# Retention with adapters: batches on opposite partition halves, and 64x64 causal score tiles

## The chip, the cores and the metric

The kernel runs on one core of one Trainium2 chip. The metric is the device time of one execution in microseconds. Three runs of the kernel before gave 205.89, 206.98 and 207.31 us; the median is 206.98 us.

## What is computed

For 8 batches, 8 heads, 576 tokens and a head size of 64, the first part is retention: `scores = (q kᵀ) / 8`, every score multiplied by `gamma_h ** (i - j)` where token j is not after token i and by zero elsewhere, and the result multiplied by v. `gamma_h = 1 - 2 ** (-5 - h)`. The 8 heads of a token side by side form a row x of 512.

The second part is a mixture of adapters on the 4608 rows x: `logits = x @ w_gate` (8 experts), the two largest logits are turned into two weights by a softmax over the two, and the output is `x + sum over the two experts of weight * (x @ A[e]) @ B[e]`, where A[e] is 512 x 16 and B[e] is 16 x 512. All inputs and the output are float32.

## The kernel before, in words

Retention is computed in chunks of 128 tokens, four full ones and a last one of 64. Because the decay factorises, `gamma ** (i - j)` is split: q carries `gamma ** i` (times the scale 1/8), v carries `gamma ** -j`, and what earlier chunks contribute is a 64 x 64 state P per batch and head, multiplied by `gamma ** 128` from chunk to chunk.

The work is cut into *units*: one chunk of one pair of batches. A *quad* is one chunk of four batches, so two units, and is what is loaded at a time: chunk 0 of batches 0 to 3, chunk 0 of batches 4 to 7, chunk 1 of batches 0 to 3, and so on. There are 16 full units and 4 half ones (the chunk of 64). In a full unit the 128 tokens lie on the 128 partitions, and the two batches lie beside each other in the free dimension.

For each unit the stages, with their lines, are:

- T (`stage_T`, L204): 16 transposes of q (L229) and 16 of k (L229), each of 64 tokens by two heads, into PSUM tiles `pt_q` and `pt_k`. VectorE moves q out and multiplies it by `aqp`, the decay and the scale (L241); ScalarE copies k out (L250).
- S (`stage_S`, L264): 16 score matmuls of kT (64 x 128) with qT (64 x 128) into four tiles `ps_s` (L291), and four VectorE products with the triangular mask `tri` into `rt` (L302). The whole 128 x 128 square of a chunk is computed, and its upper triangle is multiplied by zero.
- O (`stage_O`, L323): from the second chunk on, 16 matmuls of the state P with qT, into `px` (L359); and 16 matmuls of k with v over 128 tokens into `pu` (L373). VectorE adds the old state (L387) and GpSimd multiplies by `gamma ** 128` (L388).
- R (`stage_R`, L395): 16 matmuls of v with rt on top of `px` (L408), copied out by ScalarE as xT (L417). xT is the transposed row x.
- Z (`stage_Z`, L440): 8 matmuls of xT with A and w_gate side by side (L447) into `pz`, then the router on VectorE and ScalarE (L460 to L479), which ends with `zc`.
- B, X, Y (L501, L487, L523), for the unit before: 16 transposes of xT back into `po` (L512), two of zc into `pzt` (L493) with a ScalarE copy (L498), four matmuls with B on top of `po` (L533), four ScalarE copies to `osb` (L543) and the stores (L548).

GpSimd multiplies v by its decay in place (`scale_v`, L197). A half unit has two batches on opposite partition halves, 64 tokens each, and does the same stages in smaller shapes (L341, L426, L437).

A float32 matmul appears in the trace as two instructions, a transpose as one. A tile form such as 64*128 is the number of rows and columns of the TensorE array that an instruction uses; instructions on different parts of the array can overlap.

The order of the work is written out in the loop at the end of the kernel (L561 to L576):

```python
        if t % 2 == 0:
            issue(t // 2 + 2)
        stage_S(t)
        if t + 1 < NU:
            scale_v(t + 1)
        stage_O(t)
        stage_R(t)
        if t + 1 < NU:
            stage_T(t + 1)
        if t > 0:
            stage_B(t - 1)
            stage_X(t - 1)
        stage_Z(t)
```

A scheduler of the language puts each engine's instructions into their order, mostly the written one, and inserts the waits. All PSUM tiles come from one pool `pp` of eight banks. All loads of q, k and v and all stores are issued from SyncE's queue (SP), in one order: the loads of a quad are issued two quads ahead (`issue`, L158), into one of three sets of buffers. A full quad is three DMAs of 1 MB (L127); the first quad is loaded in two halves of 512 KB per tensor, with the constants and the adapters' weights (L101, L105) between them; the last chunk's DMAs write 64 partitions each (L148).

Of the kernel before, what the change touches and what calls it, by code (L numbers as in the profile page):

```python
# [18 lines left out]
def kernel(  # L19
# [17 lines left out]
    NP = B // 2  # L37
    NFULL = S // 128
    LH = S - 128 * NFULL
    QUAD = 4  # L40
    NQ = B // QUAD

    scale = 1.0 / float(np.sqrt(Dh))
    gam = 1.0 - 2.0 ** (-5.0 - np.arange(H, dtype=np.float64))
    jj = np.arange(128, dtype=np.float64)

    ident32_np = np.eye(128, dtype=np.float32)
    tri_np = (jj[None, :] >= jj[:, None]).astype(np.float32)
    j64 = np.arange(128) % 64
    i64 = np.arange(64)  # L50
    trih_np = (i64[None, :] >= j64[:, None]).astype(np.float32)
    aqp_np = np.zeros((128, HP, 128), dtype=np.float32)
    g128_np = np.zeros((128, HP), dtype=np.float32)
    for hp in range(HP):
        for ho in range(2):
            g = gam[2 * hp + ho]
            aqp_np[64 * ho : 64 * ho + 64, hp, :] = scale * g ** jj[None, :]
            g128_np[64 * ho : 64 * ho + 64, hp] = g**128.0
    gv_np = np.stack([gam[h] ** (-jj) for h in range(H)], axis=1).astype(np.float32)
    gvh_np = np.stack([gam[h] ** (-j64.astype(np.float64)) for h in range(H)], axis=1).astype(  # L60
        np.float32
    )
    i64_np = np.concatenate([np.eye(64), np.eye(64)], axis=0).astype(np.float32)
    first_np = i64_np
    rest_np = np.concatenate(
        [ident32_np, tri_np, trih_np, gv_np, gvh_np, g128_np], axis=1
    ).astype(np.float32)
    NPK = rest_np.shape[1]
    dr_first = nc.inline_tensor(first_np, "c_first")
    dr_rest = nc.inline_tensor(rest_np, "c_rest")  # L70
    dr_aqp = nc.inline_tensor(aqp_np, "c_aqp")
# [5 lines left out]
    pp = ctx.enter_context(tc.tile_pool(name="pp", bufs=8, space=bass.MemoryType.PSUM))  # L77

    id64 = cpool.tile([128, 64], FP32, tag="id64", name="id64")
# [5 lines left out]
    aqp = cpool.tile([128, HP, 128], FP32, tag="aqp", name="aqp")  # L85
    ident32 = pack[:, 0:128]
    tri = pack[:, 128:256]
    trih = pack[:, 256:320]
    gv = pack[:, 320 : 320 + H]
    gvh = pack[:, 320 + H : 320 + 2 * H]  # L90
    g128 = pack[:, 320 + 2 * H : 320 + 2 * H + HP]

    AW = []
    for par in range(2):
        AW.append(cpool.tile([128, HP, ER + E], FP32, tag=f"AW{par}", name=f"AW{par}"))
    Bcat = cpool.tile([128, Dm], FP16, tag="Bcat", name="Bcat")
    ident16 = cpool.tile([128, 128], FP16, tag="ident16", name="ident16")

# [12 lines left out]

    nat = {}

    def issue_full(c, qd, split):
        tiles = []
        for src, tag in ((q, "q32"), (k, "k32"), (v, "v32")):
            tiles.append((src, iop.tile([128, QUAD * H, Dh], FP32, tag=tag, name=tag)))
        parts = ((0, 2), (2, 4)) if split else ((0, 4),)
        for lo, hi in parts:
            for src, tl in tiles:  # L120
                if split and lo == 0 and src is k:
                    nc.sync.dma_start(out=aqp, in_=dr_aqp.ap())
                if split and lo == 0 and src is v:
                    nc.sync.dma_start(out=pack, in_=dr_rest.ap())
                if split and lo == 2 and src is q:
                    load_moe()
                nc.sync.dma_start(  # L127
                    out=tl[:, lo * H : hi * H, :],
                    in_=src[
                        QUAD * qd + lo : QUAD * qd + hi, :, 128 * c : 128 * c + 128, :  # L130
                    ].rearrange("b h j d -> j (b h) d"),
                )
        for half in range(2):
            nat[(c, 2 * qd + half)] = [
                tl[:, half * 2 * H : half * 2 * H + 2 * H, :] for _, tl in tiles
            ]

    def issue_half(qd):

        s0 = 128 * NFULL  # L140
        tiles = []
        for src, tag in ((q, "q32"), (k, "k32"), (v, "v32")):
            tiles.append((src, iop.tile([128, QUAD * H, Dh], FP32, tag=tag, name=tag)))
        for slot in range(2):
            for src, tl in tiles:
                for par in range(2):
                    b = QUAD * qd + 2 * slot + par
                    nc.sync.dma_start(  # L148
                        out=tl[64 * par : 64 * par + LH, slot * H : slot * H + H, :],
                        in_=src[b, :, s0 : s0 + LH, :].rearrange("h j d -> j h d"),  # L150
                    )
            nat[(NFULL, 2 * qd + slot)] = [
                tl[:, slot * H : slot * H + H, :] for _, tl in tiles
            ]

    quads = [(c, qd) for c in range(NFULL + 1) for qd in range(NQ)]

    def issue(n):  # L158
        if n < len(quads):
            c, qd = quads[n]  # L160
            if c < NFULL:
                issue_full(c, qd, n == 0)
            else:
                issue_half(qd)
# [155 lines left out]
    def col(full, b, ho):  # L320
        return (ho ^ b) if full else ho
# [289 lines left out]
```

## Time and profile before

| what | value |
|---|---|
| median of three runs | 206.98 us |
| the profiled execution's own time | 207.16 us |
| its span, first to last instruction | 205.1 us |
| TensorE matmul busy | 183.8 us (90%), 3564 instructions |
| TensorE weight loads | 166.2 us, 3564 instructions |
| VectorE busy | 108.7 us (53%) |
| ScalarE busy | 76.6 us (37%) |
| GpSimd busy | 59.6 us (29%) |
| DMA, q1 (loads and stores) | 38.50 MB, 68.0% of 16 engines' span |

The profile is of one execution. PE is TensorE's matmuls, PEld its weight loads, DVE VectorE, ACT ScalarE, POOL GpSimd, SP SyncE. The rows of digits cut the span into 40 slices; a digit is a busy share in tenths, and PEclk is the TensorE clock that was granted. In the chain that ended last, a line gives the start, the length, the engine, the tile written and the source line with the number of instructions; the chain goes from each piece of work to what released it. In the timeline an x32 stands for 32 instructions merged into one line, and the length goes to the modelled end of the last one. In the table of stretches, each line has the stretch, its length, the busy time of PE, PEld, DVE, ACT and POOL with their instruction counts, the granted clock, the DMA share and GB/s.

### The profile page before, as it was taken

The page shows a single profiled execution, that of the slowest core. Times are in us where ns is not written, and L with a number is a line of the kernel's source. Part 1 is how long each engine was busy: PE and PEld are TensorE (multiplying, and loading weights), DVE is VectorE, ACT ScalarE, POOL GpSimd, SP SyncE. Part 2 cuts the span into 40 slices and gives each one's busy share as a digit, 9 for nine tenths or more (in the row PEclk, how much of TensorE's full clock was granted, in tenths as well). Part 3 has the DMA queues.
Part 4 walks back from the last instruction along what each step waited for, and adds up shares of the span by engine and source line. Part 5 has one row for each costly group of instructions (what it writes and reads, how often), then busy time and mean ns, then how long its engine had stood idle before and what let it go on. Part 6 is the DMA issues. An engine that isn't in the chain of part 4 may idle for free.

```text
span 205.1 us, 8039 instructions
## 1 busy us (share of the span) xinstructions
PE 183.8 (90%) x3564; PEld 166.2 (81%) x3564; DVE 108.7 (53%) x286; ACT 76.6 (37%) x206; POOL 59.6 (29%) x60
## 2 busy tenths in 40 slices
PE   0476989799999999999999999999999999999950
PEld 0376969598999999999999999999999899888830
DVE  0226364937374746465656565656565655456630
ACT  2022324153525262625252525253434344454430
POOL 1144323521818202727202720643222402000000
PEclk9999999999999999999999999999999999999997
DMA  5989999799998988991799969756545311222222
GB/s 114 277 109 246 249 243 280 194 290 290 253 319 245 261 249 274 284 297 36 220 286 254 266 215 293 213 145 179 150 118 158 96 51 60 101 79 76 58 47 61
DMA packets 57442, 39.14 MB, mean 191 GB/s; under 512 B 30912, under 2 KB 52672, under 8 KB 57408
## 3 DMA queue, kind: packets, MB, share of 16 engines
q1 hardware_dynamic: 57264, 38.50, 68.0%
q8 instruction: 28, 0.46, 0.9%
q0 software_dynamic: 144, 0.13, 0.4%
q14 instruction: 6, 0.05, 0.1%
HBM read 29.32 MB, written 9.44 MB: 189 GB/s over the span
## 4 chain that ended last, share of the span: by engine, by line
PE 72%; SPq 9%; DVE 7%; DMA 5%; ACT 3%; issue 1%; ACTq 0%
PE pz L447 16%; PE px L408 12%; PE ps_s L291 12%; PE pu L373 6%; PE px L359 6%; PE pt_q L229 5%; DMA k<-in_k_dram 5%; PE po L512 4%; SPq L127 4%; PE pt_k L229 4%; PE po L533 3%; DVE rt L302 2%; PE px L426 2%; ACT osb L543 2%; SPq L101 2%; PE pzt L493 2%
## 5 line engine op out<-in xcount | busy, mean ns | idle before, releaser
L197 POOL TENSOR_TENSOR v<-v,pack 128x512 f32<-128x512 f32 x36 | 36.6, 1042 | 28.0 <-DMA v<-in_v_dram 28.0
L417 ACT COPY xT<-px 128x512 f32<-128x512 f32 x32 | 18.7, 585 | 66.0 <-PE px L408 66.0
L388 POOL TENSOR_TENSOR P<-pn,gdec 128x512 f32<-128x512 f32 x16 | 20.3, 1271 | 75.3 <-DVE pn L387 58.9
L302 DVE TENSOR_TENSOR rt<-ps_s,pack 128x512 f32<-128x512 f32 x64 | 39.7, 682 | 4.2 <-PE ps_s L291 4.2
L291 PE MATMUL ps_s<-qT,kT 64*128 64x128 f32 (+1 forms) x640 | 37.4, 275 | 1.2 <-ACT kT L250 1.2
L447 PE MATMUL pz<-AW,xT 128*128 128x136 f32 x288 | 37.8, 283 | 0.4 <-ACT zT L498 0.4
L291 PEld LDWEIGHTS ps_s<-qT,kT 64*128 64x128 f32 (+1 forms) x640 | 33.7, 184 | 5.3 <-DVE lg L460 3.4
L241 DVE TENSOR_TENSOR qT<-pt_q,aqp 128x512 f32<-128x512 f32 x32 | 20.6, 686 | 31.1 <-PE pt_q L229 31.1
L408 PE MATMUL px<-rt,v 128*64 128x128 f32 x512 | 34.1, 275 | 1.8 <-DVE rt L302 1.7
L447 PEld LDWEIGHTS pz<-AW,xT 128*128 128x128 f32 x288 | 34.7, 190 | 0.6 <-ACT zT L498 0.5
L543 ACT COPY osb<-po 128x256 f32<-128x256 f32 x72 | 23.1, 375 | 25.8 <-PE po L533 25.8
L408 PEld LDWEIGHTS px<-rt,v 128*64 128x64 f32 x512 | 29.0, 137 | 3.8 <-DVE rt L302 2.5
L250 ACT COPY kT<-pt_k 128x512 f32<-128x512 f32 x32 | 17.2, 589 | 19.2 <-PE pt_k L229 19.2
L460 DVE COPY lg<-pz 128x16 f32<-128x16 f32 (+1 forms) x20 | 3.5, 173 | 35.0 <-PE pz L447 35.0
L229 PE MATMUL pt_q<-id,q 64*128 64x64 f32 x288 | 13.6, 234 | 6.7 <-DMA q<-in_q_dram 6.7
L373 PE MATMUL pu<-v,k 128*64 128x64 f32 x512 | 18.9, 225 | 0.0
L373 PEld LDWEIGHTS pu<-v,k 128*64 128x64 f32 x512 | 16.5, 137 | 2.7 <-issue 2.1
L229 PEld LDWEIGHTS pt_q<-id,q 64*128 64x128 f32 x288 | 10.8, 142 | 9.6 <-issue 9.4
L229 PE MATMUL pt_k<-id,k 64*128 64x64 f32 x288 | 12.8, 228 | 3.4 <-DMA k<-in_k_dram 3.4
L473 DVE SCALAR_TENSOR_TENSOR cm<-lg,m,sg 128x8 f32<-128x8 f32 x36 | 9.9, 294 | 8.8 <-ACT sg L468 8.8
L229 PEld LDWEIGHTS pt_k<-id,k 64*128 64x128 f32 x288 | 10.9, 143 | 3.8 <-issue 1.7
L359 PE MATMUL px<-qT,P 64*64 64x128 f32 x384 | 13.2, 275 | 0.0
(34 smaller groups left out, 139.9 us busy)
## 6 DMA issues: line engine op xcount, KB each, us to landing
out_dram<-osb SPq DMA_DIRECT2D x32, 256.0 KB, 3.2
q<-in_q_dram SPq DMA_DIRECT2D x2, 512.0 KB, 5.0
k<-in_k_dram SPq DMA_DIRECT2D x2, 512.0 KB, 6.0
v<-in_v_dram SPq DMA_DIRECT2D x2, 512.0 KB, 5.4
q<-in_q_dram SPq DMA_DIRECT2D x8, 128.0 KB, 3.4
k<-in_k_dram SPq DMA_DIRECT2D x8, 128.0 KB, 3.3
v<-in_v_dram SPq DMA_DIRECT2D x8, 128.0 KB, 4.1
out_dram<-osb SPq DMA_DIRECT2D x8, 128.0 KB, 2.4
```

Source lines behind the costliest of these rows:

```text
L197: nc.gpsimd.tensor_tensor(out=v32[:, b * H : b * H + H, :], in0=v32[:, b * H : b * H + H, :], in1=g.unsqueeze(2).broadcast_to((128, H, Dh) ...
L229: nc.tensor.matmul(ps[r][:, hp, b, :] if full else ps[r][:, hp, :], lhsT=src[sl, b * H + 2 * hp : b * H + 2 * hp + 2, :], rhs=id64[sl, :], ...
L241: nc.vector.tensor_tensor(out=o, in0=ps[r], in1=aqp[:, :, 64 * r : 64 * r + 64] .unsqueeze(2) .broadcast_to((128, HP, 2, 64)), op=ALU.mult,)
L291: nc.tensor.matmul(o, lhsT=kT[sl, hp, b, :], rhs=qT[sl, hp, b, :], start=(a == 0 and (b == 0 or not full)), stop=True, skip_group_check=True,)
L302: nc.vector.tensor_tensor(out=r.rearrange("p a b i -> p (a b) i"), in0=ps[ho].rearrange("p a b i -> p (a b) i"), in1=tri.unsqueeze(1).broa ...
L359: nc.tensor.matmul(px[b][64 * cc : 64 * cc + 64, hp, :], lhsT=P[bp][64 * ho : 64 * ho + 64, hp, b, :], rhs=qT[64 * ho : 64 * ho + 64, hp, ...
L373: nc.tensor.matmul(pu[64 * ho : 64 * ho + 64, hp, b, :], lhsT=s["k"][:, b * H + h, :], rhs=s["v"][:, b * H + h, :], start=(hp == 0 and b = ...
L388: nc.gpsimd.tensor_tensor(out=pf, in0=pn, in1=gdec.rearrange("p a b d -> p (a b d)"), op=ALU.mult,)
L408: nc.tensor.matmul(px[b][64 * cc : 64 * cc + 64, hp, :], lhsT=s["v"][:, b * H + h, :], rhs=rt[h][:, b, :], start=(c == 0 and hp == 0), sto ...
L417: nc.scalar.copy(out=xt, in_=px[b])
L447: nc.tensor.matmul(pz[:, b, :], lhsT=xts[b][:, dt, :], rhs=AW[b][:, dt, :], start=(dt == 0), stop=(dt == HP - 1), skip_group_check=True,)
L543: nc.scalar.copy(out=osb[:, b, :, cc ^ b, :], in_=po[cc][:, b])
```

## The change

The kernel is rewritten around another layout. The two batches of a full unit now lie on opposite partition halves: batch b has partitions 64b to 64b+63. A chunk of 128 tokens is two parts e = 0, 1 (early and late 64 tokens), each in a tile of its own. A unit is still two batches of one chunk (of the four batches of a quad, one from the first two and one from the last two). In the last chunk of 64 tokens, a unit is now all four batches of a quad, so that there are two such units instead of four.

- Scores: early keys against all 128 queries of the chunk (64 x 128) and late keys against the 64 late queries (64 x 64); the tile of late keys and early queries is not computed. Mask tiles are `triE` and `tri`; the results are `re` and `rl`.
- Retention: the same two shapes, early v with re, late v with rl.
- State update: early and late k with v, 64 tokens each, accumulated; the state per batch is written to a new buffer each time.
- The decay and scale of the query are taken off q and put on the output: q is copied out by ScalarE, and xT is a VectorE product of px with `asc`.
- Loads: per tensor and quad four DMAs (two parts, two halves of the partitions), 256 KB each; in the first quad eight of 128 KB.
- The order: state product (now `stage_Q`), S, T of the next unit, B of the last, R, state update (`stage_U`), X, Z, Y.
- PSUM: `px` has a pool of two banks of its own, everything else shares six.

The diff, cut to its core:

```diff
-    pp = ctx.enter_context(tc.tile_pool(name="pp", bufs=8, space=bass.MemoryType.PSUM))
+    pxp = ctx.enter_context(tc.tile_pool(name="pxp", bufs=2, space=bass.MemoryType.PSUM))
+    pp = ctx.enter_context(tc.tile_pool(name="pp", bufs=6, space=bass.MemoryType.PSUM))
...
+        def load(dst, srct, t0, s):
+            for b in range(2):
+                bs = QUAD * qd + 2 * b + s.start
                 nc.sync.dma_start(
+                    out=dst[64 * b : 64 * b + 64, s].rearrange("p s h d -> p (s h) d"),
+                    in_=srct[bs : bs + s.stop - s.start, :, t0 : t0 + L, :].rearrange(
+                        "s h p d -> p (s h) d"
+                    ),
+                )
+
+        for s in (slice(0, 1), slice(1, 2)) if first else (slice(0, 2),):
+            if first and s.start == 1:
+                nc.sync.dma_start(out=asc[0], in_=dr_asc.ap())
+                load_moe()
+            for e in range(ne):
+                load(qt[e], q, C * c + L * e, s)
...
+    def stage_Q(t):
...
+        for hp in range(HP):
+            for x in range(n):
+                for ho in range(2):
+                    for b in range(2):
+                        nc.tensor.matmul(
+                            px[b][rows(ho ^ b), hp, w * x : w * x + w],
+                            lhsT=P[(qd, sl + x)][b][rows(ho), hp, :],
+                            rhs=s["qT"][rows(ho), b, hp, w * x : w * x + w],
...
     def stage_S(t):
...
+        pe = [pp.tile([128, HP, C], FP32, tag="pb", name=f"pe{ho}") for ho in range(2)]
+        pl = [pp.tile([128, HP, L], FP32, tag="pb", name=f"pl{ho}") for ho in range(2)] if full else []
+        for x in range(2):
+            for hp in range(HP):
                 for b in range(2):
                     for ho in range(2):
+                        if x == 1 and full:
+                            o = pl[ho][rows(b), hp, :]
...
+                        i0 = L * x
+                        i1 = C if full else L * x + L
                         nc.tensor.matmul(
                             o,
+                            lhsT=s["kT"][rows(ho), b, hp, L * x : L * x + L],
+                            rhs=s["qT"][rows(ho), b, hp, i0:i1],
...
+                nc.vector.tensor_tensor(
+                    out=r, in0=pe[ho],
+                    in1=triE.unsqueeze(1).broadcast_to((128, HP, C)), op=ALU.mult,
+                )
...
     def stage_R(t):
...
+        for x, (e, sx) in enumerate(parts(t)):
+            for hp in range(HP):
+                for ho in range(2):
+                    for b in range(2):
+                        if full and x == 1:
+                            w = s["rl"][ho][rows(b), hp, :]
+                        elif full:
+                            w = s["re"][ho][rows(b), hp, :]
...
                         nc.tensor.matmul(
+                            px[b][rows(ho ^ b), hp, L * x : C if full else L * x + L],
+                            lhsT=vt[e][rows(b), sx, 2 * hp + ho, :],
+                            rhs=w,
...
+                nc.vector.tensor_tensor(out=xt, in0=px[b], in1=asc[b], op=ALU.mult)
...
+    def stage_U(t):
...
+        pu = [pp.tile([128, HP, Dh], FP32, tag="pb", name="pu") for _ in range(2)]
+        for hp in range(HP):
+            for e in range(2):
+                for ho in range(2):
+                    for b in range(2):
+                        h = 2 * hp + ho
                         nc.tensor.matmul(
+                            pu[b][rows(ho), hp, :],
+                            lhsT=kt[e][rows(b), sl, h, :],
+                            rhs=vt[e][rows(b), sl, h, :],
+                            start=(hp == 0 and e == 0),
+                            stop=(e == 1),
...
+    for ho in range(2):
+        nc.gpsimd.tensor_copy(out=asc[1][rows(ho)], in_=asc[0][rows(1 - ho)])
...
     for t in range(NU):
-        if t % 2 == 0:
-            issue(t // 2 + 2)
-        stage_S(t)
+        if units[t][2] == 0:
+            issue(quads.index(units[t][:2]) + 2)
         if t + 1 < NU:
             scale_v(t + 1)
-        stage_O(t)
-        stage_R(t)
+        stage_Q(t)
+        stage_S(t)
         if t + 1 < NU:
             stage_T(t + 1)
         if t > 0:
             stage_B(t - 1)
+        stage_R(t)
+        stage_U(t)
+        if t > 0:
             stage_X(t - 1)
         stage_Z(t)
```

## The prediction

> **What bounds the kernel now.** I read the page first, then the chain that ended last, then TensorE's timeline, the waits, and the stretches with their DMA share.
>
> ```profile
> PE 183.8 (90%) x3564; PEld 166.2 (81%) x3564; DVE 108.7 (53%) x286; ACT 76.6 (37%) x206; POOL 59.6 (29%) x60
> ...
> PEclk9999999999999999999999999999999999999997
> DMA  5989999799998988991799969756545311222222
> ```
>
> TensorE is busy throughout at a full granted clock. The DMA row shows a second resource near its limit in the first 130 us. One unit of the steady state, from the chain:
>
> ```profile
> 75.74 1.99 PE ps_s L291 x32
> 77.72 1.03 PE px L359 x32
> 78.76 1.08 PE pu L373 x32
> 79.84 1.75 PE px L408 x32
> 81.59 0.64 PE pt_q L229 x15
> 82.23 0.49 PE pt_k L229 x16
> 82.72 0.50 PE po L512 x16
> 83.43 1.91 PE pz L447 x16
> 85.34 0.44 PE po L533 x4
> 85.78 1.99 PE ps_s L291 x32
> ```
>
> From 75.74 to 85.78 is 10.04 us, and every piece is TensorE: here only TensorE's own work sets the pace. This holds from 55.65 (unit 4) to 176.0 (end of unit 15). Before that, loads of q and k end TensorE's waits (the page's chain gives 5% to them); after it come four half units and the tail.
>
> **What a tile form costs.** TensorE's timeline, start of a stage to start of the next:
>
> ```profile
> 65.62 2.06 PE L291 MATMUL ps_s<-qT,kT 64*128 64x128 f32 x32
> 67.61 1.10 PE L359 MATMUL px<-qT,P 64*64 64x128 f32 x32
> 68.64 1.15 PE L373 MATMUL pu<-v,k 128*64 128x64 f32 x32
> 69.62 1.92 PE L408 MATMUL px<-rt,v 128*64 128x128 f32 x32
> 71.47 0.71 PE L229 MATMUL pt_q<-id,q 64*128 64x64 f32 x16
> ...
> 181.69 0.69 PE L291 MATMUL ps_s<-qT,kT 64*64 64x64 f32 x32
> 182.20 1.11 PE L341 MATMUL pq<-qT,P 64*64 64x64 f32 x32
> ```
>
> So 32 instructions (16 fp32 matmuls, two passes each) cost 1.99 us as 64*128 with 128 columns, 1.85 as 128*64 with 128, 1.03 as 64*64 with 128, and 0.51 as 64*64 with 64 columns, if neighbours sit on all four quarters of the array. L341, which uses two quarters, needs 0.9 for the same 32. I went through the new index expressions: scores, retention, state update and state product all walk the four quarters in each group of four.
>
> **The change on TensorE, one full unit.** Scores: 1.99 becomes 1.03 + 0.51 = 1.54 (−0.45). Retention: 1.85 becomes 1.54 (−0.31). State update: 64 passes of 64*64 with 64 columns instead of 32 of 128*64: 2 × 0.51 = 1.02 against 0.98 (+0.04). State product, transposes, gate and output keep counts and forms. Sum −0.72. The starts also show about 0.15 us lost at each change of form; the new order has one such change less, and two halves of a stage share one, so up to 0.3 more may go. TensorE's work is then 9.0 to 9.3.
>
> [...]
>
> **A new wait: PSUM.** Eight shared banks become six plus two reserved for px. In a unit the new order wants four banks for scores, four for transposes, two for po, in that order. At the end of the scores the transposes of the next unit find two free (the last po and pz); the second k bank needs re1 evicted. In the unit from 75.67 VectorE ends its router work (zc) at 77.24, so 1.57 after the unit's start. The scores' first half ends at about 1.03 + 1.03 = 2.06 less the shared boundary, 1.9; re0 and re1 then take the pace of L302 (four in 2.48 us, 0.62 each), ending at about 3.4. The scores end at 2.4 to 2.5, q's transposes at 3.0: TensorE waits some 0.4 to 0.5. Behind it in TensorE's queue stand B, R, U, Z and all of the unit, so the wait is paid in full. Bounds: nothing, if banks fall better; 1.4, if the transposes must wait for all four score evictions (2 × 0.62 + 2 × 0.42, the latter from the 128x256 L310). I take 0.45, in the middle of this count. The retention itself waits for nothing: T and B stand between scores and R, more than rl0 and rl1 need. The xT product (a 128x512 two-input VectorE operation, 0.69 as L241, instead of ACT's 0.585 copy) is hidden behind U and X (1.1 us) before Z; without this cover it would cost 0.7. VectorE's sum per unit is about as before (two 0.69 moved to ACT with q, two 0.69 come with xT, four 0.62 become two 0.62 and two 0.42, one 0.69 becomes two 0.42); ACT swaps two copies for two. GpSimd's P product is split and stays far off the path (58.9 us idle before L388). Its new start work (a memset, a copy of tri, two asc copies of about 0.64 as L182) stands ahead of scale_v(1), which waits until about 25 us for v anyway.
>
> With work of 9.05 (9.32 less about 0.27 of boundaries) and 0.45 of wait a unit takes 9.5: −0.54, times twelve = **−6.5 us**.
>
> **Half units and tail.** Before: from 176.01 to the last pz's end at 196.85 is 20.8, then 8.3 to 205.1. After, two units of four 64-token batches: each 0.51 × 6 for Q, S and R, T 1.1 (first only), B 0.5, X 0.1, Z 1.9, Y 0.44, boundaries 0.4, that is 7.5 and 6.4. No U stands between R and Z, so xT shows: 0.7 each; in the last unit no T covers the evictions: 0.8. Together 15.4 to 16. The tail has twice the width: two more osb copies (0.65) and more router operations (0.5): 9.4. 29.1 becomes about 25: **−4 us**. That is −3.3 if the waits double.
>
> **Loads.** A 1 MB load per tensor becomes four of 256 KB into 64 rows each; issuing them costs SP 0.63 each (L148's 128 KB form), 7.6 us per quad of 19. SP's order (loads of quad n+2, then stores) is the same. What they cost the DMA engines, from three stretches:
>
> ```profile
> 15.00:20.00 5.00, 3.80 (x82) 3.38 (x80) 3.15 (x5) 1.17 (x2) 2.54 (x3) 1.00 1.05 237
> ...
> 40.00:45.00 5.00, 4.83 (x86) 4.51 (x86) 2.08 (x4) 2.52 (x5) 1.27 (x1) 1.00 1.00 284
> 130.00:135.00 5.00, 5.00 (x99) 4.76 (x95) 1.98 (x3) 2.52 (x5) 5.00 (x5) 1.00 0.71 162
> ```
>
> The last two columns are DMA share and GB/s. The first holds the 512 KB loads, the second 1 MB ones, the third the 64-row ones of 128 KB. At full share they give 226, 284 and 228 GB/s. The nearest row to the new loads is the third. A quad's 3.15 MB then takes 13.8 us (11.1 before), its stores 2.8 (1.05 MB; from 170 to 180 us, with stores alone, 59 GB/s at a share of 0.16, that is 370): 16.6 of the 19.0 us that TensorE takes per quad. Hidden, but with 2.4 us of room; before it was 13.9 of 20.1.
>
> [...]
>
> The start feels it. SP needs 24 issues of 0.63 for quad 0 instead of 6. Up to k of its second half it is 20 of them (12.6), the A and gate loads (5.5 in SP's timeline) and some 1.9 for the start and constants: issued at 20, landed at 22 (before 20.3). Then v, and q and k of quad 1 at 228 GB/s (0.5 + 2.1 MB, 11.5 us): 33 (TensorE's wait for it ended at 30.50). The transposes stand ahead of R now, so unit 1's R, U, Z and Y (5.6) follow: unit 2 begins at 39 instead of 34.2. Units 2 and 3 have no Q, find their loads there, and no longer wait for rt: about 8.6 each instead of 10.5 and more. Unit 4 starts at 56 to 56.5, against 55.65: **+0.5** (bounds −2 and +5).
>
> **Sum** against the profiled execution's own 207.16 (span 205.1 and 2.06 around it): −6.5 − 4 + 0.5 = −10, so 197.1; it lies 0.18 above the median, so **196.9 us**. What a measurement here tells from no change is about 1%, 205 to 209.
>
> **Rivals.**
> - PSUM paces the unit (13%): every transposition waits for all score evictions, 9.05 + 1.4 = 10.45, no gain in the middle; with the tail's −3.3 and the start's +2, 12 × 0.4 = +5: 210. With 1.0 of wait, no gain and no loss, 206. For: all ten banks of a unit in a row ask for six. Against: VectorE is 53% busy.
> - The loads pace it; this one ends on the other side (15%). Place: the 64-row loads of quads 2 to 7, six quads from k of quad 1 at 34 to k of quad 7; behind it remain 50 us of TensorE work and 2 around. 207 is reached at 20.2 us per quad, a load rate of 181 GB/s; at the 162 actually moved in the third stretch it is 22.2 per quad and 219 us. For: the DMA row is at 9 already. Against: 228 per full share.
> - The narrow passes don't overlap by four in the new order (5%; the state product's order of quarters, same rows in succession, is seen nowhere): at L341's 0.9 per 32, four groups, +1.6 per unit: 9.5 + 1.6 = 11.1, 216 us.
> - No wait at all and all the boundary gain (12%): 9.0 per unit, 191.
>
> The forecast has 55%, spanning 192 to 203. **Chances**: faster by over 1% 0.68, within 0.08, slower 0.24. Range 190 to 213: it leaves out most of the loads' case and the third rival.
>
> **What would show it.** Right: from the second quad of chunk 1 on, a unit of about 9.5 us in the chain; scores and retention at 1.5 each; a short wait of kT's transposes for VectorE's re; the DMA share near 0.9 without TensorE waiting for q or k after 50 us. Wrong: waits for DMA at pqT or pkT in the middle, 32 narrow passes near 0.9, or stages in another order on TensorE, which would move the wait.

## The result and the profile after

The changed kernel takes 256.93 us (median of four, 254.11 to 262.63) against 207.14 for the kernel before (205.89 to 207.66): 1.228 times as long, 95% interval 1.2185 to 1.2375, or 47 us. The prediction was 196.9 with a range up to 213. Every case in it, the rivals too, is too fast by 35 us or more. Ratios, intervals and the differences between kernels below leave out executions more than 1.5% above their kernel's quickest (here 259.67 and 262.63, at a granted clock of 0.942 and 0.916 against 0.968 and 0.967), medians are over all of them, and the profiles of `e6`, `e10`, `e11`, `e16` and `e17` are of such slower executions.

The page of the changed kernel, the same lines as before:

```profile
PE 211.1 (84%) x5100; PEld 183.3 (73%) x5100; DVE 104.7 (42%) x282; ACT 76.7 (30%) x200; POOL 57.5 (23%) x72
...
PEclk9996599999999999999999999999999999999995
DMA  5887798998998980689339940879178004831233
```

TensorE has idle time in the steady state now, and the DMA engines nearly stand still for whole slices (the zeros, 0 to 18 GB/s on the page), so the loads don't pace the middle.

Where the time sits can be read from the start of the scores of unit 4, the start of those of the first unit of the last chunk, and the end of the span:

| | unit 4 | last chunk | per unit between (12) | rest |
|---|---|---|---|---|
| before | 55.6 | 176.0 | 10.04 | 29.0 |
| after | 68.4 | 224.9 | 13.04 | 27.1 |

Of 46.9 us in the spans, 12.8 are lost before the scores of unit 4, 36.0 in the twelve units, and 2.0 are won at the end. (The state product Q, 0.9 us, stands ahead of the scores now, so it is counted with what precedes them.)

TensorE's timeline of the changed kernel over one pair of units, each line with its start, length and instructions:

```profile
133.41 1.10 PE L213 MATMUL px<-qT,P 64*64 64x128 f32 x32
134.33 1.05 PE L238 MATMUL pe<-qT,kT 64*64 64x128 f32 x32
135.21 0.64 PE L238 MATMUL pl<-qT,kT 64*64 64x64 f32 x32
135.78 0.27 PE L186 MATMUL pqT<-id,q 64*128 64x64 f32 x2
136.19 0.43 PE L285 MATMUL px<-re,v 64*64 64x128 f32 x2
136.55 0.64 PE L186 MATMUL pqT<-id,q 64*128 64x64 f32 x7
137.12 0.99 PE L285 MATMUL px<-re,v 64*64 64x128 f32 x27
...
138.50 0.64 PE L186 MATMUL pqT<-id,q 64*128 64x64 f32 x7
...
140.30 1.47 PE L213 MATMUL px<-qT,P 64*64 64x128 f32 x26 [0.89 <-DVE xT L297]
...
144.04 0.64 PE L186 MATMUL pkT<-id,k 64*128 64x64 f32 x7
...
145.42 0.27 PE L360 MATMUL pzt<-ident,zc 128*128 128x128 f16 x2 [0.46 <-ACT kT L195]
...
147.60 0.64 PE L186 MATMUL pkT<-id,k 64*128 64x64 f32 x7
...
151.46 0.69 PE L238 MATMUL pl<-qT,kT 64*64 64x64 f32 x30 [1.46 <-DVE zc L405]
...
160.22 1.10 PE L213 MATMUL px<-qT,P 64*64 64x128 f32 x32
```

From 133.41 to 160.22 are two units. The narrow passes run as predicted: the 32 of Q, all starting within 0.84 us, and 32 of `pl` from 135.21 to 135.78. But **this is not the order written in the kernel**. The next unit's transposes, written as one block of 32 that alternates between the partition halves, are cut into groups of seven of one half; the next unit's state product stands at 140.30, ahead of this unit's U; k's transposes are spread as far as past Z. In a group of seven one transpose starts 62 ns after the other, 70 with the change of form ahead of the group (31 ns where the halves alternate). And there are waits, in these two units each for a PSUM bank. TensorE's list of waits for this kernel, total, times and longest:

```profile
PE pl L238 <- DVE zc L405: 7.3, 5, 1.5
PE pqT L186 <- DMA q<-in_q_dram: 6.9, 4, 5.3
PE px L213 <- DVE xT L297: 4.2, 6, 0.9
PE pzt L360 <- ACT kT L195: 3.2, 7, 0.5
```

No operand of `pl` comes from zc: `pl` was given the bank of the unit before's `pz`, as the built program's list of banks has it. The waits for q are all early ones. The largest wait was lengthened on VectorE (175.00 to 177.74 in its timeline) beside GpSimd's scaling of v, which runs from 173.75 for 4.05 us:

```profile
175.00 0.81 DVE L389 SCALAR_TENSOR_TENSOR ns<-m 128x2 f32<-128x2 f32 x1
176.18 1.64 DVE L399 SCALAR_TENSOR_TENSOR cm<-lg,m,sg 128x8 f32<-128x8 f32 x2 [0.37 <-ACT sg L394]
177.74 0.47 DVE L405 TENSOR_TENSOR zc<-pz,cm 128x128 f16<-128x128 f32 x2
```

In the unit before it the same two steps took 0.16 and 0.42.

Where the 3.0 us more per unit come from can be counted in the trace, from start to start over the twelve units. Idle time of TensorE is 1.5 us per unit. The 32 transposes of q and k take 2.2 us instead of 1.0. Scores, retention, state product and state update take 5.9 us as before, where the prediction has 0.7 less; that they lose it because they are cut into pieces among other forms is likely, but not tried. The rest takes 0.3 more.

### The profile page after: what moved, and what is told of

Same layout as the page of the kernel before. It is cut to its first block, busy times and chain, and to the rows that moved or that the text cites. A ratio compares the mean times of both kernels' runs of the same rounds, so it can differ in the third digit from the quotient of the medians.

```text
span 251.9 us, 11229 instructions
## 1 busy us (share of the span) xinstructions
PE 211.1 (84%) x5100; PEld 183.3 (73%) x5100; DVE 104.7 (42%) x282; ACT 76.7 (30%) x200; POOL 57.5 (23%) x72
## 4 chain that ended last, share of the span: by engine, by line
PE 63%; DVE 17%; SPq 7%; ACT 6%; issue 3%; DMA 1%; ACTq 0%; DVEq 0%
PE pz L373 15%; PE px L285 12%; PE px L213 8%; PE pu L318 7%; PE pkT L186 5%; PE pqT L186 5%; DVE cm L399 5%; SPq L126 5%; PE po L345 4%; DVE re L250 4%; PE pe L238 3%; ACT qT L195 3%; DVE ns L389 2%; DVE xT L297 2%; PE po L421 2%
## 5 line engine op out<-in xcount | busy, mean ns | idle before, releaser
L297 DVE TENSOR_TENSOR xT<-px,asc 128x512 f32<-128x512 f32 x32 | 20.6, 686 | 43.8 <-PE px L285 43.8
L373 PEld LDWEIGHTS pz<-AW,xT 128*128 128x128 f32 x288 | 36.4, 198 | 2.2 <-ACT zT L365 1.1
L195 ACT COPY kT<-pkT 128x512 f32<-128x512 f32 x36 | 20.4, 595 | 55.6 <-PE pkT L186 55.5
L186 PE MATMUL pqT<-id,q 64*128 64x64 f32 x288 | 24.4, 238 | 7.6 <-DMA q<-in_q_dram 6.9
L285 PE MATMUL px<-re,v 64*64 64x128 f32 (+1 forms) x640 | 25.8, 272 | 4.1 <-issue 1.5
L186 PE MATMUL pkT<-id,k 64*128 64x64 f32 x288 | 27.0, 242 | 1.6 <-DMA k<-in_k_dram 1.1
L213 PE MATMUL px<-qT,P 64*64 64x128 f32 (+1 forms) x512 | 21.0, 264 | 5.0 <-DVE xT L297 4.2
L250 DVE TENSOR_TENSOR re<-pe,triE 128x512 f32<-128x512 f32 x32 | 20.5, 681 | 8.2 <-PE pe L238 8.1
L318 PE MATMUL pu<-v,k 64*64 64x64 f32 x1024 | 23.6, 227 | 0.2 <-ACT qT L195 0.2
L238 PE MATMUL pe<-qT,kT 64*64 64x128 f32 (+1 forms) x640 | 22.8, 271 | 0.9 <-ACT kT L195 0.9
L318 PEld LDWEIGHTS pu<-v,k 64*64 64x64 f32 x1024 | 20.3, 139 | 1.5 <-ACT qT L195 0.3
```

The lines of the kernel that those rows point to most:

```text
L186: nc.tensor.matmul(ps[b][:, hp, x, :], lhsT=lhs, rhs=id64[rows(b), :], is_transpose=True, start=True, stop=True,)
L195: nc.scalar.copy(out=dst[:, b].rearrange("p a (x i) -> p a x i", x=2), in_=ps[b])
L213: nc.tensor.matmul(px[b][rows(ho ^ b), hp, w * x : w * x + w], lhsT=P[(qd, sl + x)][b][rows(ho), hp, :], rhs=s["qT"][rows(ho), b, hp, w * ...
L238: nc.tensor.matmul(o, lhsT=s["kT"][rows(ho), b, hp, L * x : L * x + L], rhs=s["qT"][rows(ho), b, hp, i0:i1], start=(hp == 0 and (x == 0 or ...
L250: nc.vector.tensor_tensor(out=r, in0=pe[ho], in1=triE.unsqueeze(1).broadcast_to((128, HP, C)), op=ALU.mult,)
L285: nc.tensor.matmul(px[b][rows(ho ^ b), hp, L * x : C if full else L * x + L], lhsT=vt[e][rows(b), sx, 2 * hp + ho, :], rhs=w, start=(c == ...
```

## The experiments

The theories, as they stand in the expectations: **A**, six shared banks are too few; **B**, the new order (T and B ahead of R) costs; **C**, loads into 64 rows are slow; **D**, TensorE's order, laid out by the scheduler around the four separate load pieces, costs.

### Banks, order and loads, one at a time

`e1_8banks`: the changed kernel with px in one pool of eight with all others.

```diff
-    pxp = ctx.enter_context(tc.tile_pool(name="pxp", bufs=2, space=bass.MemoryType.PSUM))
-    pp = ctx.enter_context(tc.tile_pool(name="pp", bufs=6, space=bass.MemoryType.PSUM))
+    pp = ctx.enter_context(tc.tile_pool(name="pp", bufs=8, space=bass.MemoryType.PSUM))
```

> The changed kernel, with px taken from the shared pool again: eight shared banks instead of six and two. Theory A (too few PSUM banks: a matmul group waits for the eviction of another, and the scheduler splits the transposes): most of the 50 us come back, 210 to 225. Theory B (the new order, transposes and po ahead of the retention): stays at 245 or more. Theory C (the 64-row loads): stays at 250 or more.

232.89 us (231.59 to 235.4), 1.1208 of before [1.115, 1.1266]; 11.56 per unit. Transposes still stand in sevens. A gives 22 of the 47 us.

`e2_order` and `e3_both`: U and R written ahead of T and B (Q, S, U, R, T, B, X, Z, Y), with six and two banks, and with eight.

```diff
         stage_S(t)
+        stage_U(t)
+        stage_R(t)
         if t + 1 < NU:
             stage_T(t + 1)
...
-        stage_R(t)
-        stage_U(t)
```

> The changed kernel with six and two banks, but with the order of before behind the scores: state update, retention, then transposes, po and pzt. Theory A: 240 to 260, the banks are as few as they were. Theory B: 205 to 215. Theory C: 250 or more.

> The changed kernel with eight shared banks and the order of before behind the scores. Theory A: about as e1, 205 to 225; Theory B: about as e2, 205 to 215; if it is far under both, banks and order act together, about 198 as predicted for the change; Theory C: 245 or more.

278.12 (ratio 1.3381 [1.3292, 1.3471]) and 254.76 (1.2227 [1.2117, 1.2338]): 21 to 23 us slower than with the new order. B falls, as far as the scheduler lays out the order, and so did the idea that a better written order gives a better order on the engine.

`e4_before_6plus2`: the kernel before with px in a pool of two and six shared banks. `e5_before_64row`: the kernel before, loaded in pieces of 64 rows (256 KB, in the first quad 128 KB).

```diff
-    pp = ctx.enter_context(tc.tile_pool(name="pp", bufs=8, space=bass.MemoryType.PSUM))
+    pxp = ctx.enter_context(tc.tile_pool(name="pxp", bufs=2, space=bass.MemoryType.PSUM))
+    pp = ctx.enter_context(tc.tile_pool(name="pp", bufs=6, space=bass.MemoryType.PSUM))
...
-            pp.tile([128, HP, L], FP32, tag="pb", name=f"px{b}") for b in range(2)
+            pxp.tile([128, HP, L], FP32, tag="px", name=f"px{b}") for b in range(2)
```

```diff
+                step = 1 if split else 2
+                for r in range(2):
+                    for l2 in range(lo, hi, step):
+                        nc.sync.dma_start(
+                            out=tl[64 * r : 64 * r + 64, l2 * H : (l2 + step) * H, :],
...
```

> The kernel before with px in a pool of two banks of its own and six shared for all else. Theory A: slower than before by 10 us or more, since its stages need about as many tiles at a time as the changed ones. Theory B and C: 207, within 2 us.

> The kernel before, with every load of a full chunk cut as the change cuts it: four DMAs of 256 KB into 64 rows in place of one of 1 MB (eight of 128 KB for the first quad). Theory C (the loads themselves are slow): 225 or more. Theory D (the loads only matter through the order in which TensorE's instructions were written down: its transposes wait for four pieces, and the order around them is laid out for late pieces; here that order is nearly the one of before): 207 to 212.

212.69 (1.0257 [1.0211, 1.0302]), 10.44 per unit; and 214.31 (1.0335 [1.025, 1.042]), 10.21 per unit with unit 4 at 59.5. Six banks cost 5 us in the old order, and the small loads some 6, most of it in the start. C is no cause of the middle.

### Around the loads: three runs that missed

To let the scheduler see the loads earlier, they are issued three quads ahead into four sets of buffers: with eight banks (`e6_8banks_ahead`), with six and two (`e7_ahead`), and with eight and the scores in two groups of two tiles of 384 columns (`e8_grouped`).

```diff
-    iop = ctx.enter_context(tc.tile_pool(name="io", bufs=3))
+    iop = ctx.enter_context(tc.tile_pool(name="io", bufs=4))
...
+    issue(2)
...
-            issue(quads.index(units[t][:2]) + 2)
+            issue(quads.index(units[t][:2]) + 3)
```

The grouping of `e8_grouped`, beside that:

```diff
-        pe = [pp.tile([128, HP, C], FP32, tag="pb", name=f"pe{ho}") for ho in range(2)]
...
+        G = 2
+        for g in range(HP // G):
+            ps = [
+                pp.tile([128, G, C + L] if full else [128, G, C], FP32, tag="pb", name=f"ps{ho}")
+                for ho in range(2)
+            ]
```

> The changed kernel with eight shared banks (as the first experiment, 232.9) and loads issued three quads ahead into four sets of buffers instead of two ahead into three. The transposes of a unit then stand together in TensorE's order in every other unit, and in pieces of 8 in the rest. Theory D: 205 to 220. Theory A alone (banks): 230 to 235, as without it. Theory C: 230 or more.

> The changed kernel with its six and two banks, and only the loads issued three quads ahead. Theory D: 10 to 25 us less than the change, 230 to 245; Theory A alone: 255, as the change. Theory C: 250 to 260.

> As the kernel with eight shared banks and loads three quads ahead, and the scores written in two groups of two head pairs, early and late scores of a group in one bank (four tiles of 384 columns instead of two of 512 and two of 256): two banks are enough at a time. Theory A and D together: 197 to 207, the prediction's unit of 9.0 to 9.5 us in the middle. If something else paces the unit: 215 or more.

282.23 (1.3309 [1.3186, 1.3431]), 292.5 (1.3903 [1.3802, 1.4004]) and 277.38 (1.3277 [1.3164, 1.339]): far outside. An earlier load made the kernel 44 us slower with eight banks and 35 with six and two; `e8_grouped` has no partner without it. What it was comes below.

### TensorE held in the written order

Each of TensorE's instructions is tied behind the one written before it; this sets the order alone and adds no wait for completion: in the unit of e9 below `pe` starts at 130.40, while `px` runs to 130.57. With eight banks (`e9_8banks_written`) and with the changed kernel's own six and two (`e10_6plus2_written`).

```diff
+    def mm(*a, **kw):
+        tc.keep_in_program_order(nc.tensor.matmul(*a, **kw))
```

> The changed kernel with eight shared banks, and TensorE's instructions held in exactly the order in which the kernel writes them (Q, S, T, B, R, U, X, Z, Y, each whole; transposes alternate between the partition halves). Nothing else differs from the eight-bank run (232.9 us). Theory D (TensorE's order, laid out around the separate load pieces, is the other half of the loss): a unit falls from 11.5 to 9.3-9.9 us (about 8.8 of work by the rows, with transposes at 31 ns instead of 70, and 0.5-1 us of bank waits), so 205-214 us in all, with the start still 5 us late. Rival (the order costs nothing, the waits come from somewhere else, or holding the order makes TensorE wait for late loads): 228 us or more.

> The changed kernel as it is, six shared banks and two for px, with TensorE's instructions held in the written order. It tells whether the banks matter by themselves or only through the order. Theory A and D together: the unit waits for banks once more than with eight, 9.9-10.8 us per unit, 212-224 us. If D alone made the loss: the same as with eight banks within 2 us. If A alone: 250 us or more.

221.6 (218.97 to 224.19; 1.0545 [1.0462, 1.0627]) and 225.75 (1.0727 [1.0613, 1.084]). The order alone takes 31 us off the changed kernel, and with it the banks are worth 4, no longer 22. One unit of e9 in TensorE's timeline (all matmuls have the line of the helper):

```profile
129.47 1.10 PE L154 MATMUL px<-qT,P 64*64 64x128 f32 x32
130.40 1.05 PE L154 MATMUL pe<-qT,kT 64*64 64x128 f32 x32
131.27 1.09 PE L154 MATMUL pl<-qT,kT 64*64 64x64 f32 x32
132.29 0.71 PE L154 MATMUL pqT<-id,q 64*128 64x64 f32 x16
132.85 0.71 PE L154 MATMUL pkT<-id,k 64*128 64x64 f32 x16
133.40 0.83 PE L154 MATMUL po<-id,xT 64*128 64x64 f32 x16
134.15 1.10 PE L154 MATMUL px<-re,v 64*64 64x128 f32 x32
135.07 0.64 PE L154 MATMUL px<-rl,v 64*64 64x64 f32 x32
135.54 1.11 PE L154 MATMUL pu<-v,k 64*64 64x64 f32 x64
136.59 0.28 PE L154 MATMUL pzt<-ident,zc 128*128 128x128 f16 x2
136.71 2.07 PE L154 MATMUL pz<-AW,xT 128*128 128x136 f32 x16
138.62 0.60 PE L154 MATMUL po<-Bcat,zT 128*128 128x256 f16 x4
139.15 0.88 PE L154 MATMUL px<-qT,P 64*64 64x128 f32 x23
```

It takes 9.68 us, 0.44 of it a hole inside `pl` (which takes 0.57 elsewhere). In size that is near the unit that was predicted, 9.05 and 0.45, but the wait is another one. Behind the hole stands the router of the unit before, in whose `pz` bank half of `pl` lies:

```profile
131.05 0.47 DVE L407 TENSOR_TENSOR zc<-pz,cm 128x128 f16<-128x128 f32 x2
```

The wait that the prediction counted, k's transposes for `re`, comes in six of the twelve units, with 0.23 to 0.31 us. And the unit shown is the second shortest: the twelve run from 9.67 to 12.04 and take 10.61 on average, and e9 missed its own expectation by 8 us. What is in the other units shows in TensorE's list of waits in e9:

```profile
PE pu L154 <- issue: 7.2, 7, 2.0
...
PE pkT L154 <- DVE re L252: 1.5, 6, 0.3
```

and in its DMA queues (packets, MB, share), first e9, then the kernel before:

```profile
q8 instruction: 40, 0.66, 1.3%
```

```profile
q8 instruction: 28, 0.46, 0.9%
```

For 9.2 us TensorE stands still without a wait that the profile knows (7.2 in U, 2.0 in px and pz). The queue that the profile names `q8 instruction` moves 40 packets of 16 KB (0.66 MB) instead of 28 (0.46 MB); TensorE has 5100 matmul instructions instead of 3564. In the trace of e9 such a packet starts at 80.05, 90.52, 100.25, 112.80, 123.64 and 155.56 us and lands 0.9 to 1.9 later; the stops end at 82.68, 92.82, 102.64, 115.96, 126.07 and 157.89, each 1.3 to 1.6 after a landing. Of e9's twelve stops eleven end so, and in all eight kernels with the order held 77 of 90 end 1.2 to 1.65 us after a landing, though in e9's steady part the packets land some 4 to 6 us apart. The kernel before has no such stop in its list. The number of packets isn't enough to make them: the changed kernel as the scheduler ordered it moves the same 40 and stops for 2.1 us, and `e1_8banks` for 3.4.

`e11_written_vscale_dve`: e9 with the scaling of v on VectorE.

```diff
-            nc.gpsimd.tensor_tensor(
+            nc.vector.tensor_tensor(
                 out=vv,
```

> Eight banks, written order, and the scaling of v moved from GpSimd to VectorE (36 products of 128x512, about 0.7 us each, 1.4 us per unit on VectorE). Theory: the long router instructions (0.82 us instead of 0.2 for each gate product, in every second unit) come from GpSimd's scaling beside them; all of them are then 0.2-0.3 us. If the late router was still on TensorE's path: 3 to 8 us faster than with GpSimd scaling. Rival (the added VectorE work delays the masks or the products after it): 0 to 8 us slower.

223.49 (1.0709 [1.0626, 1.0791]), some 3 us slower than e9, on its rival's side. Each gate product now takes 0.225 to 0.266 us, where the changed kernel had up to 1.08 and e9 up to 0.64, so the long ones do come from GpSimd's work beside them. But VectorE has 36 products of 0.69 more, and TensorE's list of waits now has 4.1 us for `re` at q's transposes, which e9's lacks.

`e12_before_serialT`: in the kernel before, the loop over the partition half outside.

```diff
-            for hp in range(HP):
-                for b in range(2 if full else 1):
-                    for r in range(2):
+            for r in range(2):
+                for hp in range(HP):
+                    for b in range(2 if full else 1):
```

> The kernel before, with the loops of the q and k transposes turned round, so that eight transposes of one partition half follow each other and then eight of the other; nothing else moves. The price of this order by itself: 32 transposes per unit at 70 instead of 31 ns, 1.25 us per unit, 17 to 22 us for sixteen units and the half ones: 224-229 us. Rival (the 70 ns have another cause, or neighbours fill the gap): 207-211 us.

213.15 (1.025 [1.0188, 1.0312]): 0.4 us per unit, a third of what was expected. The price was too high, because the last transposes of one half overlap the first of the next, q's with k's and k's with `po`: q's and k's start some 43 ns apart on the whole. At 62 to 70 ns stands a group between other work, as in the changed kernel.

### What is left

`e13_half_update`: e9 with a state update from the early half alone.

```diff
-            for e in range(2):
+            for e in range(1):
```

> Eight banks, written order, and the state update computed from the early 64 tokens of each chunk alone: 32 instead of 64 instructions per unit, the late tokens' contribution to the state is left out. In the eight-bank run with written order TensorE stood still for about 9 us without waiting for anything that the profile shows, mostly inside the state update, and each of these stops ends 1.3 to 1.6 us after a 16-KB transfer on the queue that carries instructions. Theory F (TensorE runs out of instructions where 128 narrow ones follow each other, retention and update): work falls by 0.46 us per unit, 7 us in all, and the unexplained stops fall from 9 us to 4 or less, so 207-211 us. Rival (the stops have another cause, tied to time or to the DMAs): only the work goes, the stops stay at 8-9 us, 213-216 us.

214.2 (1.0318 [1.0256, 1.038]). The stops fall from 9.2 to 5.1 us, towards theory F's 4 or less, the time only as its rival has it: without half of U, `pz` waits for xT (2.4 us), and banks come later (`pl` for zc 1.7, pqT for re 1.2). That fewer instructions in a row mean fewer stops is not shown by this pair alone: the next run, with e9's instructions and only its first loads issued otherwise, stops for 12.1 us. Nor is the time they cost settled.

`e15_written_2queues`: e9 with 12 of the first quad's 24 loads from ScalarE's queue.

```diff
-                nc.sync.dma_start(
+                (nc.scalar if first and b else nc.sync).dma_start(
```

> Eight banks, written order, and in the first quad the loads of the second partition half issued from ScalarE's queue instead of SyncE's (12 of 24). Theory C2 (the late start, unit 4 at 64.2 instead of 55.7 us, is paced by issuing 35 loads at 0.64 us one after the other): unit 4 begins 3-6 us earlier, 215-219 us. Rival (the bytes pace the start, at some 222 GB/s): within 1.5 us of the run with one queue, 221.6 us.

216.44 (1.0404 [1.0327, 1.0482]); the scores of unit 4 at 60.6 instead of 65.0. That much of the start was paced by one queue's issues.

`e14_written_ahead`: e9 with the loads three quads ahead.

> Eight banks, written order, loads issued three quads ahead into four sets of buffers. The same prefetch without the held order made the kernel 49 us slower than without it (282 against 233 us). Theory D (that loss was only in TensorE's order, which the scheduler laid out differently around the loads): with the order held the deeper prefetch costs nothing, 217-224 us. Rival (the deeper prefetch itself costs, by its DMA traffic or the memory it fills): 235 us or more.

287.48 (282.95 to 289.75), 1.39 of before by the medians. So theory D alone doesn't explain e6 to e8: with the order held the prefetch still costs 65 us. TensorE in one unit of it:

```profile
173.45 1.10 PE L154 MATMUL pe<-qT,kT 64*64 64x128 f32 x30 [0.68 <-DVE zc L407]
175.32 0.33 PE L154 MATMUL pl<-qT,kT 64*64 64x64 f32 x2 [0.78 <-DVE re L252]
175.92 0.69 PE L154 MATMUL pl<-qT,kT 64*64 64x64 f32 x30 [0.27 <-DVE re L252]
177.13 1.04 PE L154 MATMUL pqT<-id,q 64*128 64x64 f32 x16 [0.52 <-DVE rl L265]
178.84 1.60 PE L154 MATMUL pkT<-id,k 64*128 64x64 f32 x16 [0.68 <-ACT qT L197]
181.07 1.60 PE L154 MATMUL po<-id,xT 64*128 64x64 f32 x16 [0.63 <-ACT kT L197]
```

Every stage waits for the one just before it to be moved out of PSUM, as if there were two banks. There are: the built programs list a bank for each tile, and in units 7, 9, 11 and 13 of e14 ten tiles take turns in two. (One unit of e9 and unit 9 of e14, order of first use; tile:bank. In unit 11, whose timeline stands above, the two are 7 and 2.)

```
e9   px:5 px:6 pe0:7 pe1:3 pl0:1 pl1:4 pqT:7 pqT:0 pkT:3 pkT:2 po0:1 po1:4 pu:7 pu:0
e14  px:6 px:2 pe0:3 pe1:0 pl0:3 pl1:0 pqT:3 pqT:0 pkT:3 pkT:0 po0:3 po1:0 pu:6 pu:2
```

These four units take 21.4 to 23.5 us each, the ones between them 12.8 to 14.3. The program of e6 has the same pattern, in one unit with banks 3 and 1. Which tile gets which bank is chosen by the scheduler, and it changes when the loads move.

`e16_ahead_pinned`: e14 with the banks written by hand.

```diff
+    BK = {"px": "01", "pe": "23", "pl": "45", "pqT": "67", "pkT": "23",
+          "po": "45", "pu": "67", "pzt": "2", "pz": "3"}
...
-        pe = [pp.tile([128, HP, C], FP32, tag="pb", name=f"pe{ho}") for ho in range(2)]
+        pe = [pp.tile([128, HP, C], FP32, tag=f"b{BK['pe'][ho]}", name=f"pe{ho}") for ho in range(2)]
```

> The last run's slow prefetch kernel (written order, loads three quads ahead, 287.5 us) with one edit: every PSUM tile gets a bank written by hand (px and two more of eight each: px 0-1, pe 2-3, pl 4-5, q's transposes 6-7, k's 2-3, po 4-5, pu 6-7, pzt 2, pz 3) instead of the bank that the scheduler takes from the pool. In that kernel's program the scheduler gives two banks in turn to all ten tiles of every second unit (pe, pl, pqT, pkT and po all in banks 3 and 0) while the other banks lie idle. Theory G (the choice of banks makes the deeper prefetch slow, not the loads or the memory): TensorE's waits for pe, pl, px and pqT on VectorE's masks and router go, and the time falls to 214-224 us. Rival (the prefetch's traffic or buffers): 270 us or more.

242.35 (1.1672 [1.1606, 1.1739]): 43 of the 65 us are gone with nothing changed but the banks. The rest is, by the list of waits, mostly my own choice; its first line in e16:

```profile
PE pe L155 <- DVE zc L408: 19.6, 17, 2.3
```

I had put `pz` and the next unit's `pe1` into bank 3, so the next scores wait for the router. The banks explain two thirds of the loss; that they also explain the remainder is read from this list, and no run with other banks and the prefetch has tried it.

`e17_pinned_U_early`: e15 with hand-written banks and U between S and T.

```diff
+    BK = {"px": "01", "pe": "23", "pl": "45", "pqT": "23", "pkT": "45",
+          "po": "67", "pu": "67", "pzt": "2", "pz": "4"}
...
         stage_S(t)
+        stage_U(t)
         if t + 1 < NU:
             stage_T(t + 1)
+        stage_R(t)
         if t > 0:
             stage_B(t - 1)
-        stage_R(t)
-        stage_U(t)
```

> What the runs point to, in one kernel: held order, banks by hand, half of the first quad's loads from ScalarE's queue (as in the two-queue run, 216.4 us), and the state update moved between S and T, where it covers the masks (order Q, S, U, T, R, B, X, Z, Y; banks px 0-1, pe 2-3, pl 4-5, pu 6-7, pqT 2-3, pkT 4-5, po 6-7, pzt 2, pz 4). By the rows a unit has 9.2 us of work, 0.25 of wait for xT ahead of Z, and 0.6 of instruction supply: 10.0; unit 4 begins at 59; twelve units, 25.3 to the end and 2 around it: 206, range 202-211. If the waits for masks and router (pkT, pl, cm in the chain) were not what the order costs: as the two-queue run, 214-218 us.

222.91 (1.0584 [1.0509, 1.066]), 3 us slower than e15. The waits for masks went as meant (a unit from 109.72 to 119.51 has none), but the scores of unit 4 began at 64.3, the unexplained stops stood at 16.9 us (7.4 in px, 4.5 in pkT, 1.7 in pu, 1.5 in po, 1.3 in pzt, 0.5 in pqT) instead of 12.1 in e15, and my banks put `pl` behind the router again (3.0 us for zc: `pz` and half of `pl` share a bank). Behind one stop of 2.2 us ahead of k's transposes the granted clock was 0.5 from 103.5 to 106.9 us, and four passes took 213 ns instead of 109. Q, S and U in a row are 160 instructions in 3.3 us; that this made more stops fits theory F, but the run doesn't single it out.

`e18_before_adapterq`: the kernel before, with the adapters' and gate's loads from ScalarE's queue.

```diff
     def load_moe():
         for dt in range(HP):
-            nc.sync.dma_start(
+            nc.scalar.dma_start(
...
-        nc.sync.dma_start(
+        nc.scalar.dma_start(
```

> The kernel before, with the five loads of the adapters' and gate's weights issued from ScalarE's queue at the start instead of between the two halves of the first quad on SyncE's (7.69 to 13.23 us in its queue, a stretch in which the DMAs moved 114 GB/s against 237 and more around it). What the two-queue run won in the changed layout (unit 4 at 60.6 instead of 65.0) should be won in part here: the later loads come 2 to 5 us earlier, unit 4 begins at 52-54 instead of 55.65, and the kernel takes 203-206 us. Rival (the bytes pace the start, or the small loads now delay the first q and k by as much): 206.5-208 us.

206.15 (205.13 to 206.97) against 207.96 for the kernel before beside it, 0.9894 [0.9845, 0.9943]. Unit 4 begins at 54.0 instead of 55.6. It is the fastest kernel of the study, by 1%.

## Why the prediction was wrong, step by step

- **What bounds the kernel before**: right, 10.04 us per unit of TensorE's own work.
- **Tile forms and the unit's work, 9.0 to 9.3**: the prices of the narrow passes are right. Groups of four start 109 ns (128 columns) and 58 ns (64 columns) apart, that is 0.87 and 0.46 per 32, in the state product's order of quarters too; at 64 columns that is 14.5 ns per pass. The sum of 9.0 to 9.3 holds only where the stages stay whole, as in the unit of e9 (9.24).
- **The new wait, 0.45 per unit, and "transposes ... keep counts and forms", no cost**: this is the step that failed. The wait began with "in a unit the new order wants four banks for scores, four for transposes, two for po, in that order", and took the written order for TensorE's, and every free bank as one that the next tile may have. As the scheduler laid out the order and the banks, a unit took 13.0: 1.5 of idle time instead of 0.45, transposes of q and k at 2.2 instead of 1.0, and no gain in the narrow stages. Holding the order alone gives back 31 of 47 us (e10), the eight banks alone 22 (e1), both 35 (e9); the two overlap, since the order decides which banks are asked for at once. That a unit of e9 waits 0.44, as forecast, is luck, because it waits for another tile. The text named "stages in another order" as what would make it wrong, but gave it no chance and no price.
- **The twelve units, −6.5**: not reached in any run. In e9 they take 10.61 on average. Without their stops (7.6 us in all) it would be 9.98, the pace of the kernel before.
- **Half units and tail, −4**: −1.0 in the changed kernel, counted from the last chunk's first state product, and −3.6 with the order held (25.5 to the end in e9, about 25 forecast). Right but for the same cause.
- **Start, +0.5 (bounds −2 and +5)**: +8.5 with the order held (unit 4 begins with Q at 64.1), of which the two queues give back 4.4. The term was mis-sized at three places: k of quad 1 landed at 36.4, not 33; behind it came 8.8 us to unit 2, not 5.6, as the granted clock was 0.5 from 35.9 to 42.7; and units 2 and 3 took 9.1 and 9.8, not 8.6.
- **Loads**: right. From 30 to 35 us the changed kernel moved 235 GB/s at a share of 1.04, so 226 at full share (228 taken). TensorE of the changed kernel waits for no load after 50 us.
- **Not in the prediction**: the stops, 2.1 us in the changed kernel, 9.2 in e9, 5 to 17 in all kernels with the order held. That TensorE runs out of instructions in them is argued from the times of packets and stops, not shown; e13 agrees in the stops and not in the sum.
- **Rivals**: PSUM was the right place, but the rival was capped at one order of stages (10.45 per unit). The narrow passes' rival and the loads' are out.

Open: why the held order with eight banks keeps some 9 us more than the kernel before even with two queues. In e15 the start is 4.1 later, the end 3.3 shorter, and the twelve units together 7.9 longer. The stops among these sum to 8.1, but waits for masks and banks stand there too, and no run takes the stops away.

## What to carry to other kernels

Where a scheduler orders an engine and hands out PSUM banks, an edit of the loads, of a pool or of the order written can change both everywhere: read the built program's order and its tile-to-bank list before pricing a wait, and hold both by hand where a kernel lives on one engine. A tile narrowed to save columns can raise the count of instructions (here from 3564 to 5100), and this may have a price of its own where many stand in a row (e9's stops sum to 9.2 us; their cause is argued, not shown). Work a cost out for the isolated group and the group among neighbours separately: 70 and 43 ns per transpose here.

## What the hardware showed that was not expected

- TensorE had stops of up to 2.5 us (e10), most of them in Q, R and U, where up to 128 narrow instructions follow each other; with the order held 77 of 90 end 1.2 to 1.65 us after a 16-KB instruction packet lands. There are none in the kernel before (3564 instructions, 28 packets); with 5100 and 40 they sum to 2.1 us in the changed kernel, 9.2 in e9, 12.1 in e15.
- In the changed kernel a VectorE product of 128x8 in SBUF took 0.58 to 1.08 us where it ran beside GpSimd's 128x512 product (14 of 36) and 0.23 otherwise; with that product on VectorE (e11) none was over 0.27.
- The granted clock was 0.862 on the mean in e14, 0.930 in e16, 0.976 in e9 and 0.995 in the kernel before. In these traces it is 1.0 or 0.5, and stretches at 0.5 ahead of the tail lasted 6.83 us in e9, 10.24 in the changed kernel and up to 17.07 in e14. In e14 they cover 58 us of the twelve units, in e16 14, so part of what the banks cost came through the clock: four instructions of `pz` take 907 ns in such stretches of e14 and 464 in e9. The mean clock did not follow the busy share here: e17's is 0.981 with TensorE 79% busy, e9's 0.976 with 83%. What sets the grant was not tried.
